# Weight units of a fused attention and two-MLP kernel handled in pairs instead of one by one

## The chip, the cores and the metric

One core of one Trainium2 chip runs the whole program. The metric is the device time of one execution in microseconds (us); lower is better. The core's engines work side by side, each through its own list of instructions in order: TensorE (PE, matrix products, with its weight loads as PEld), VectorE (DVE), ScalarE (ACT), GpSimd (POOL), and SyncE (SP), which here issues most of the transfers (DMAs) between the chip's main memory (HBM) and the core's on-chip memory. Products land in PSUM and are evacuated by ACT or DVE.

## The reference, cut to what matters

```python
# q, k, v: (4, 12, 448, 64), all float32 inputs
q_n, k_n = rmsnorm(q, g_q), rmsnorm(k, g_k)
attn = softmax(q_n @ k_n.T / 8)              # per batch and head
x = (attn @ v) -> (1792, 768)                # 1792 = 4 batches of 448 tokens
a, b = x @ w_a, x @ w_b                      # 768 -> 1536, both
x = (a * b) @ w_out                          # 1536 -> 768
h = x @ w_in                                 # 768 -> 2048
g = max(h, 0) + alpha * min(h, 0)
out = g @ w_out2                             # 2048 -> 768
```

The weights arrive as 64-bit numbers. The kernel splits every value, activations and weights, into a float16 high part and a float16 low part and adds three products (high by high, high by low, low by high), so that float32 accuracy is kept.

## The kernel before, in words

Tokens are handled in four batches of 448 columns. Each batch goes through attention and then four stages: "a" (both first products and their gate), "y" (second product), "h" (third, with the activation), "o" (the last). The list `stages` (line 598) gives their order: a0 y0 h0 o0 a1 y1 a2 h1 o1 y2 h2 a3 o2 y3 o2 h3 o3. Attention runs ahead of the stages as a generator, `att_steps`; batch 0 of it runs alone at the start, and the rest is interleaved, so many steps per stage (`RATE`, line 1258). Three late stages (`FAST`: o2, y3, o3) use a seven-product block scheme with weights formed in advance (`form_weights`, `form_block`).

Each stage is a row of *chains*: 18 or so matmuls of 128x448 that fill one PSUM bank. Weights come in *units*, one per chain in stages a and h (128 columns by 768 rows), two per chain in y and four in o. The list `stream` (lines 715 to 723) holds all units of all stages in order. In stage a, units alternate between w_a and w_b: line 1066 loops over f and, inside, over the two matrices.

The first time a unit is used (76 units, all in a0, y0, h0 and o0), it passes four steps:

- `w_load` (line 729) fetches it as 64-bit numbers into a buffer of pool `raw`, with runs of 128 columns (1 KB).
- `w_convert` (754) turns 64 bits into float32 by an ACT activation (764), a DVE shift (767) and a DVE combine (770), and sums the squares with an ACT activation (778, with a second small ACT instruction that reads the accumulator out).
- `w_scale` (786) adds the squares of a group over the partitions by one small PE matmul into the tile `tot` (`total`, line 127) and makes a power-of-two scale by three DVE instructions (`power`, 112). A group is two units in a and h, the two or four units of a chain in y and o.
- `w_split` (825) makes the high part on ACT (831) and the low part on DVE (832), and stores both to HBM (835).

Later stages fetch the split unit back with one DMA (744), or, in `FAST` stages, formed units (738).

`advance(u)` (847) runs after each unit of the stream; the table `STEPS` (839) says how many units ahead each step goes: load 12, convert 8, scale 6, split 3; refetches go 4 ahead. The pools that matter: `raw` 5 buffers, `wf` (float32 units, also the formed ones) 6, `wh` (split units) 5, `slot` (activations, 35 of 128x2x448 float16), `tmp` 3, and three PSUM banks for chains. While `state["pin"]` holds (attention of batch 0) loads keep their written place in SP's list; most other instructions are ordered by the compiler's own scheduling pass, so the order on an engine can differ from the order in the code.

Two first tiles of attention, `early`, take two of the `raw` buffers during batch 0. The block stages take `raw` buffers for their activations (`blocks`, line 942).

Attention of batches 1 to 3 writes k and q as float16 pairs (`prep3`, `prep4`) and turns them by DMA transposes on SP (lines 355 and 358, into qT and kT), a copy makes qS (361, 362), the probabilities are turned by DMA transposes too (490, into pT), and `scores` (399) then uses kT, qT and qS on PE.

Of the kernel before, what the change touches and what calls it, by code (L numbers as in the profile page):

```python
# [8 lines left out]
F32 = mybir.dt.float32  # L9
F16 = mybir.dt.float16  # L10
# [9 lines left out]
def attention_gated_mlps_kernel(  # L20
# [24 lines left out]
    SLOTS = 35  # L45
# [25 lines left out]
    def slot32(name):  # L71
# [6 lines left out]
    kd0 = keep_p.tile([128, 2 * KB * D], F32, name="kd0")  # L78
# [15 lines left out]
    cgf = const.tile([128, KF2], F32, name="cgf")  # L94
# [8 lines left out]
        "a": const.tile([128, 2 * KF], F32, name="inv_a"),  # L103
        "y": const.tile([128, KD], F32, name="inv_y"),
        "h": const.tile([128, KF2], F32, name="inv_h"),
# [165 lines left out]
    def prep2f(g):  # L271
        d = P[g]
        kr, r = d["kr"], d["rk"]
        kd = kd0[:KP]
        d["kd"] = kd
# [341 lines left out]
    def source(kind, n, part):  # L617
        _, parts, rows = CHAINS[kind]
        w, n = {
            "a": ((w_a, w_b)[n % 2], n // 2), "y": (w_out, n), "h": (w2_in, n), "o": (w2_out, n)  # L620
        }[kind]
        w = w[:, n * 128:(n + 1) * 128]
        if parts == 1:
            return w.rearrange("(k p) f -> p k f", p=128)
# [38 lines left out]
    def form_block(kind, i, j, cols):  # L663
# [3 lines left out]
        def raw():  # L667
            return raw_p.tile([128, 784], I64, tag="raw", name="raw")

        def load():  # L670
            d["x"] = x = raw().bitcast(F16)[:, 0:8 * w].rearrange("p (q l n) -> p q l n", q=4, l=2)
# [5 lines left out]
        def whole(q):  # L677
            if q == 0:
                d["r"] = raw().bitcast(F32)[:, 0:4 * w].rearrange("p (q n) -> p q n", q=4)
# [45 lines left out]

    def size(kind):
        return CHAINS[kind][2] * 128

    def w_load(u):
# [3 lines left out]
        if key[-1] == "s":  # L733
            kind, i, (f, j), _ = key
            t = wf_p.tile([128, 768], F32, tag="wf", name="ws").bitcast(F16)
            t = t[:, 0:2 * WIDE[kind]].rearrange("p (l n) -> p l n", l=2)
            tc.keep_in_program_order(
                nc.sync.dma_start(out=t, in_=form_source(kind, i, f, j))
            )
            w16[u] = t  # L740
            return
        if key in scratch:
            t = wh_p.tile([128, 2, 768], F16, tag="w16", name="w16")[:, :, 0:n]
            nc.sync.dma_start(out=t, in_=scratch[key])
            w16[u] = t
            return
# [616 lines left out]
```

## Time and profile before

| what | value |
|---|---|
| median of 3 runs | 1222.59 us (1215.45 to 1223.43) |
| the profiled execution | 1215.08 us |
| its span from first to last instruction | 1213.0 us |
| PE busy | 1145.4 us (94%) |
| DVE busy | 816.5 us (67%) |
| ACT busy | 770.1 us (63%) |
| POOL busy | 108.2 us (9%) |
| moved by DMA | 269.78 MB, mean 222 GB/s |

Busy time is the union of the instructions of an engine. An instruction's time in the profile runs from its start until its results are written, and the next one on ACT or DVE may start before that, so the sum of the times of single instructions is more than the engine's busy time. A matmul's end is modelled.

### The profile page before, as it was taken

The numbers are of one execution on the slowest core, as the hardware profiler recorded it, in microseconds if no ns is written. First come the engines' busy times: TensorE is split into PE (matmuls) and PEld (weight loads), VectorE is DVE, ScalarE is ACT, GpSimd is POOL, SyncE is SP. The second block draws the span as 40 slices with busy tenths as digits, with TensorE's granted clock in tenths as the row PEclk, the third lists the DMA queues.
The fourth block names the chain that finished last, engine by engine and source line by source line (L and its number), as shares of the span: only waits on it lengthen the run. The fifth ranks groups of instructions, "written<-read, shape, count | busy, mean of one in ns | idle before, by whom it ended". The sixth has DMA issues, their size and how long they took to land. (4 is left out here: it accounts for less than half of the span.)

```text
span 1213.0 us, 20078 instructions
## 1 busy us (share of the span) xinstructions
PE 1145.4 (94%) x7144; PEld 650.6 (54%) x7144; DVE 816.5 (67%) x1695; ACT 770.1 (63%) x1543; POOL 108.2 (9%) x176
## 2 busy tenths in 40 slices
PE   6997999899989799998999999999999999999997
PEld 3553554445434344444445554544555558996597
DVE  7898999999899666677754376554356677523631
ACT  7998999999899666767534366564255335513532
POOL 1000000000001000000012100122200562000000
PEclk9997999999989899998999999999999999999999
DMA  7658999999999999987985677898834798873465
GB/s 190 174 163 211 315 326 329 288 298 305 309 246 308 252 237 253 248 199 173 198 225 152 159 175 164 199 222 190 228 117 135 247 299 284 272 210 107 129 188 171
DMA packets 319267, 269.78 MB, mean 222 GB/s; under 512 B 178464, under 2 KB 275232, under 8 KB 319168
## 3 DMA queue, kind: packets, MB, share of 16 engines
q1 hardware_dynamic: 311376, 246.41, 75.9%
q0 software_dynamic: 7792, 22.10, 6.3%
q8 instruction: 56, 0.92, 0.3%
q14 instruction: 43, 0.35, 0.1%
HBM read 179.77 MB, written 43.25 MB: 184 GB/s over the span
## 5 line engine op out<-in xcount | busy, mean ns | idle before, releaser
L110 PEld LDWEIGHTS <-w 128*128 128x128 f16 x4104 | 398.2, 99 | 393.5 <-issue 39.6
L110 PE MATMUL p<-x,w 128*128 128x448 f16 x1728 | 336.3, 354 | 0.5 <-DVE ab L1080 0.4
L110 PE MATMUL p<-y,w 128*128 128x448 f16 x1152 | 221.6, 352 | 1.4 <-DVE t L1187 1.3
L110 PEld LDWEIGHTS <-ws 128*128 128x128 f16 x1386 | 132.5, 98 | 3.3 <-DMA ws<-f_o_S 2.7
L110 PE MATMUL p<-ab,w 128*128 128x448 f16 x648 | 129.7, 359 | 1.3 <-ACT ab L894 1.2
L110 PE MATMUL p<-g,w 128*128 128x448 f16 x576 | 119.8, 362 | 4.6 <-ACT g L1172 3.5
L421 DVE TENSOR_REDUCE nm<-s 128x2 f32<-128x896 f32 x84 | 91.2, 1086 | 33.5 <-PE s L110 33.3
L483 ACT ACTIVATE p<-pf,ri 128x448 f16<-128x448 f32 x126 | 81.8, 665 | 35.9 <-DMA pT<-p 27.4
L484 DVE SCALAR_TENSOR_TENSOR p<-pf,ri,p 128x448 f16<-128x448 f32 x126 | 84.6, 680 | 28.1 <-ACT p L483 28.0
L110 PE MATMUL l<-g,ws 128*128 128x224 f16 x960 | 94.2, 259 | 1.8 <-DMA ws<-f_o_S 1.8
L438 ACT ACTIVATE pf<-s,nm,esc 128x448 f32<-128x448 f32 x126 | 90.0, 719 | 1.4
L832 DVE SCALAR_TENSOR_TENSOR w<-wf,sc,w 128x768 f16<-128x768 f32 (+1 forms) x76 | 70.1, 929 | 2.5 <-ACT w L831 2.1
L831 ACT ACTIVATE w<-wf,sc 128x768 f16<-128x768 f32 (+1 forms) x76 | 65.4, 869 | 2.6 <-DMA sc_h<-w 1.7
L764 ACT ACTIVATE wf<-raw 128x768 f32<-128x768 f32 (+1 forms) x76 | 63.6, 843 | 5.2 <-DMA raw<-in_moe_w_out_dram 3.2
L770 DVE SCALAR_TENSOR_TENSOR wf<-raw,wf 128x768 int32<-128x768 int32 (+1 forms) x76 | 65.7, 868 | 0.3
L1083 ACT ACTIVATE junk<-ab 128x448 bf16<-128x448 f32 x48 | 27.6, 574 | 59.8 <-DVE ab L1080 59.6
L778 ACT ACTIVATE junk<-wf 128x768 bf16<-128x768 f32 (+1 forms) x76 | 59.3, 781 | 1.3 <-DVE wf L770 1.3
L707 POOL DMA_DIRECT2D f_o_S<-raw x48 | 33.8, 807 | 292.6 <-DVE raw L703 214.0
L110 PE MATMUL s<-kT,qT 128*64 128x448 f16 x252 | 48.3, 375 | 11.6 <-DMA kT<-k 9.1
L1080 DVE SCALAR_TENSOR_TENSOR ab<-p,inv_a,t 128x448 f32<-128x448 f32 x48 | 32.5, 678 | 29.6 <-PE p L110 29.0
L110 PE MATMUL s<-early 128*128 128x448 f32 x84 | 39.6, 598 | 10.0 <-ACT pf L438 9.0
L110 PE MATMUL s<-kT,qS 128*64 128x448 f16 x252 | 46.7, 365 | 2.4 <-DMA qS<-qT 2.4
(171 smaller groups left out, 1434.1 us busy)
## 6 DMA issues: line engine op xcount, KB each, us to landing
w<-sc_a SPq DMA_DIRECT2D x72, 384.0 KB, 3.7
w<-sc_h SPq DMA_DIRECT2D x48, 384.0 KB, 3.1
raw<-in_moe_w_in_dram SPq DMA_DIRECT2D x16, 768.0 KB, 7.3
raw<-in_moe_w_out_dram SPq DMA_DIRECT2D x24, 512.0 KB, 6.1
ws<-f_o_S SPq DMA_DIRECT2D x48, 256.0 KB, 3.8
raw<-in_moe_w_a_dram SPq DMA_DIRECT2D x12, 768.0 KB, 7.3
raw<-in_moe_w_b_dram SPq DMA_DIRECT2D x12, 768.0 KB, 6.5
sc_a<-w SPq DMA_DIRECT2D x24, 384.0 KB, 7.3
```

Of the source, the lines that this page charges most:

```text
L110: nc.tensor.matmul(out=o, lhsT=a, rhs=b, start=first, stop=last)
L421: nc.vector.tensor_reduce(out=nm, in_=ps[:, :, 0:S], axis=AX.X, op=ALU.max, negate=True)
L438: nc.scalar.activation(out=pf, in_=ps[:, j, 0:S], func=AF.Exp, bias=nm[:, j:j + 1], scale=scale[j], accum_out=su[:, j:j + 1],)
L483: nc.scalar.activation(out=t[:, 0, :, 0:KP], in_=pf, func=AF.Copy, scale=r)
L484: nc.vector.scalar_tensor_tensor(out=t[:, 1, :, 0:KP], in0=pf, scalar=r, in1=t[:, 0, :, 0:KP], op0=ALU.mult, op1=ALU.subtract,)
L707: nc.gpsimd.dma_start(out=formed[kind, i, name, j][:, :, cols], in_=d["x"][:, q])
L764: nc.scalar.activation(out=t, in_=hi.bitcast(F32), func=AF.Prelu, scale=2.0 ** -112, alpha=-(2.0 ** 32))
L770: nc.vector.scalar_tensor_tensor(out=ti, in0=lo, scalar=29, in1=ti, op0=ALU.logical_shift_right, op1=ALU.bitwise_or)
L778: nc.scalar.activation(out=junk(768, size(kind)), in_=t, func=AF.Square, accum_out=sums[0][:, j:j + 1])
L831: nc.scalar.activation(out=w[:, 0], in_=t, func=AF.Copy, scale=s)
L832: nc.vector.scalar_tensor_tensor(out=w[:, 1], in0=t, scalar=s, in1=w[:, 0], op0=ALU.mult, op1=ALU.subtract)
L1080: nc.vector.scalar_tensor_tensor(out=ab, in0=ps, scalar=i, in1=t, op0=ALU.mult, op1=ALU.mult)
```

## The change

Two neighbouring units become one pair: in stages a and h two chains that lie side by side (for a: two chains of w_a, then two of w_b), in y and o two parts of the same chain. A pair has one tile in each pool, one instruction per step instead of two, and one scale. For that:

- Stages a and h fetch a raw pair by one DMA with runs of 256 columns; y and o by two DMAs into one tile. Split pairs are stored and refetched by one DMA each. Formed units of the `FAST` stages share tiles in pairs too, alternately from `wf` and `wh`, with a DMA for each.
- Stage a goes through its units as w_a, w_a, w_b, w_b, so that two `tmp` tiles are held at a time.
- Pools: `raw` 3 pairs (was 5 units), `wf` 3 pairs (was 6), `wh` 3 pairs (was 5), `slot` 33 (was 35). The two `early` tiles share one raw pair; `blocks` hands out halves of one raw pair; `form_block` takes both its tiles from one. `kd0` goes; its tile now comes from pool `one`, tag k16.
- Loads go 11 units ahead while pinned and 13 after; formed units 6 ahead (was 5). The tile that takes the unused squares is 8-bit.

The diff, cut to its core:

```diff
-    SLOTS = 35
+    SLOTS = 33
-    raw_p = ctx.enter_context(tc.tile_pool(name="raw", bufs=5))
+    raw_p = ctx.enter_context(tc.tile_pool(name="raw", bufs=3))
-    wf_p = ctx.enter_context(tc.tile_pool(name="wf", bufs=6))
-    wh_p = ctx.enter_context(tc.tile_pool(name="wh", bufs=5))
+    wf_p = ctx.enter_context(tc.tile_pool(name="wf", bufs=3))
+    wh_p = ctx.enter_context(tc.tile_pool(name="wh", bufs=3))
...
-    early = [raw_p.tile([128, 784], I64, tag="raw", name=f"early{i}").bitcast(F32) for i in range(2)]
+    early = raw_p.tile([128, 2, 784], I64, tag="raw", name="early").bitcast(F32)
+    early = [early[:, i] for i in range(2)]
...
     def source(kind, n, part):
-            "a": ((w_a, w_b)[n % 2], n // 2), ...
+            "a": ((w_a, w_b)[n // 2 % 2], n // 4 * 2 + n % 2), ...
+        if parts == 1:
+            w = w[:, n * 128:(n + 2) * 128]
+            return w.rearrange("(k p) f -> p k f", p=128)
...
     def w_load(u):
-        t = raw_p.tile([128, 784], I64, tag="raw", name="raw")[:, 0:n]
-        i = nc.sync.dma_start(out=t.rearrange("p (k f) -> p k f", f=128), in_=source(*key))
+        t = raw_p.tile([128, 2 * 784], I64, tag="raw", name="raw")[:, 0:2 * n]
+        for j, x in enumerate(members[u]):
+            if j and key[0] in "ah":
+                break
+            if key[0] in "ah":
+                at = t.rearrange("p (k f) -> p k f", f=256)
+            else:
+                at = t[:, j * n:(j + 1) * n].rearrange("p (k f) -> p k f", f=128)
+            i = nc.sync.dma_start(out=at, in_=source(*stream[x]))
...
     def w_convert(u):
-        t = wf_p.tile([128, 768], F32, tag="wf", name="wf")[:, 0:size(kind)]
+        t = wf_p.tile([128, 2 * 768], F32, tag="wf", name="wf")[:, 0:2 * size(kind)]
...
     def w_scale(u):
-        us = range(u - parts * chains + 1, u + 1)
-        sc = sm_p.tile([128, 2], F32, tag="sc", name="sc")[:, 0:chains]
-        power(total(squares.pop(u), len(us), chains), sc, iv, 2)
+        us = [u - 2, u][2 - sq.shape[1]:]
+        sc = sm_p.tile([128, 1], F32, tag="sc", name="sc")
+        power(total(sq, len(us)), sc, inv[kind][:, m:m + 1], 2)
...
     def w_split(u):
-        nc.scalar.activation(out=w[:, 0], in_=t, func=AF.Copy, scale=s)
+        nc.scalar.activation(out=hi, in_=t, func=AF.Copy, scale=s)
-        nc.sync.dma_start(out=scratch[stream[u]], in_=w)
+        nc.sync.dma_start(out=whole[stream[u]], in_=w)
...
-    STEPS = [(w_load, 12), (w_convert, 8), (w_scale, 6), (w_split, 3)]
+    STEPS = [(w_load, 11), (w_convert, 8), (w_scale, 6), (w_split, 3)]
...
     def stage_a(b):
-        for f in range(KF):
-            for w in range(2):
+        for n in range(2 * KF):
+            f, w = n // 4 * 2 + n % 2, n // 2 % 2
```

## Rows read from the trace of the kernel before

**Rows 1.** The page: busy time of two engines.
```profile
PE 1145.4 (94%) x7144; PEld 650.6 (54%) x7144; DVE 816.5 (67%) x1695; ACT 770.1 (63%) x1543; POOL 108.2 (9%) x176
```
**Rows 2.** Stretches (us): engines' busy time and instructions, granted clock, DMA share, GB/s.
```profile
core 0: us, PE busy (x) PEld busy (x) DVE busy (x) ACT busy (x) POOL busy (x), PEclk, DMA share, GB/s
36.00:116.00 80.00, 66.95 (x391) 38.90 (x388) 70.95 (x205) 76.04 (x168) 0.00 (x0) 0.92 0.61 172
...
116.00:430.00 314.00, 287.65 (x1617) 144.53 (x1617) 281.29 (x593) 288.74 (x585) 9.09 (x13) 0.97 1.09 297
...
390.00:430.00 40.00, 32.24 (x176) 15.21 (x176) 25.71 (x60) 29.24 (x65) 5.77 (x8) 0.87 1.04 256
...
560.00:1213.00 653.00, 643.53 (x4257) 393.70 (x4254) 345.32 (x614) 288.44 (x528) 92.69 (x144) 1.00 0.70 194
```
**Rows 3.** Waits of PE from 116 to 430: us in total, times, longest.
```profile
PE s L110 <- DMA kT<-k: 8.5, 3, 5.4
PE p L110 <- ACT g L1172: 3.5, 1, 3.5
PE tot L110 <- ACT sq L375: 2.3, 1, 2.3
PE tot L110 <- DVE x L535: 2.2, 2, 1.6
...
PE tot L110 <- DVE tots L135: 0.7, 1, 0.7
```
**Rows 4.** Timeline of ACT in a0: start, us, line, what.
```profile
160.54 0.95 ACT L831 ACTIVATE w<-wf,sc 128x768 f16<-128x768 f32 x1
161.37 0.86 ACT L778 ACTIVATE junk<-wf 128x768 bf16<-128x768 f32 x1
162.10 0.22 ACT L778 ACTIVATION_READ_ACCUMULATOR junk<-wf 128x1 f32 x1
162.19 0.92 ACT L764 ACTIVATE wf<-raw 128x768 f32<-128x768 f32 x1
162.98 0.65 ACT L1077 ACTIVATE t<-p,inv_a 128x448 f32<-128x448 f32 x1
```
**Rows 5.** Timeline of ACT in o0, with units of 512.
```profile
389.14 0.75 ACT L831 ACTIVATE w<-wf,sc 128x512 f16<-128x512 f32 x1
389.75 0.70 ACT L764 ACTIVATE wf<-raw 128x512 f32<-128x512 f32 x1
390.31 0.66 ACT L778 ACTIVATE junk<-wf 128x512 bf16<-128x512 f32 x1
390.83 0.24 ACT L778 ACTIVATION_READ_ACCUMULATOR junk<-wf 128x1 f32 x1
390.92 0.70 ACT L483 ACTIVATE p<-pf,ri 128x448 f16<-128x448 f32 x1
```
**Rows 6.** Timeline of DVE, in a0 and in o0.
```profile
159.52 0.95 DVE L770 SCALAR_TENSOR_TENSOR wf<-raw,wf 128x768 int32<-128x768 int32 x1
160.40 1.00 DVE L832 SCALAR_TENSOR_TENSOR w<-wf,sc,w 128x768 f16<-128x768 f32 x1
161.32 0.18 DVE L267 SCALAR_TENSOR_TENSOR r<-t,r 128x30 f32<-128x30 f32 x1
...
385.26 0.75 DVE L832 SCALAR_TENSOR_TENSOR w<-wf,sc,w 128x512 f16<-128x512 f32 x1
385.92 0.68 DVE L770 SCALAR_TENSOR_TENSOR wf<-raw,wf 128x512 int32<-128x512 int32 x1
386.53 0.68 DVE L484 SCALAR_TENSOR_TENSOR p<-pf,ri,p 128x448 f16<-128x448 f32 x1
```
**Rows 7.** Issues that write kT from 116 to 430, with issue-to-landing time.
```profile
L358 SPq DMA_TRANSPOSE kT<-k x7: 1230/2361/3911, 116.1 to 428.8; - x7
...
DMA to landing us min/median/max: 3.0/5.6/7.7
```
**Rows 8.** The same from 430 to 840, after the last unit is converted.
```profile
DMA to landing us min/median/max: 2.9/3.6/7.2
```
**Rows 9.** The page: issues by what they move, KB each, median us to landing.
```profile
w<-sc_a SPq DMA_DIRECT2D x72, 384.0 KB, 3.7
raw<-in_moe_w_a_dram SPq DMA_DIRECT2D x12, 768.0 KB, 7.3
```
**Rows 10.** Timeline of PE at the first chain of stage o1.
```profile
756.00 4.34 PE L110 MATMUL p<-g,w 128*128 128x448 f16 x22
```

More of the change, by code (lines that the diff above doesn't have):

```diff
@@ L741, in w_load @@
+            for j, x in enumerate(members[u]):
+                kind, i, (f, c), _ = stream[x]
+                w = t[:, j, 0:2 * WIDE[kind]].rearrange("p (l n) -> p l n", l=2)
+                tc.keep_in_program_order(
+                    nc.sync.dma_start(out=w, in_=form_source(kind, i, f, c))
+                )
+                w16[x] = w.rearrange("p l (k f) -> p l k f", f=128)
             return
         if key in scratch:
-            t = wh_p.tile([128, 2, 768], F16, tag="w16", name="w16")[:, :, 0:n]
@@ new lines, in w_load @@
+            nc.sync.dma_start(out=t, in_=whole[key])
+            give(u, t)
+            return
+        t = raw_p.tile([128, 2 * 784], I64, tag="raw", name="raw")[:, 0:2 * n]
+        whole[key] = hbm.tile(
+            [128, 2, 2 * n] if key[0] in "ah" else [128, 2, 2, n], F16, name=f"sc_{key[0]}{key[1]}_{key[2]}"
+        )
+        for j, x in enumerate(members[u]):
+            scratch[stream[x]] = None if key[0] in "ah" else whole[key][:, j]
+            if j and key[0] in "ah":
+                break
+            if key[0] in "ah":
+                at = t.rearrange("p (k f) -> p k f", f=256)
+            else:
+                at = t[:, j * n:(j + 1) * n].rearrange("p (k f) -> p k f", f=128)
+            i = nc.sync.dma_start(out=at, in_=source(*stream[x]))
+            if state["pin"]:
+                tc.keep_in_program_order(i)
@@ L751, in w_load @@
         raws[u] = t
-        scratch[key] = hbm.tile([128, 2, n], F16, name=f"sc_{key[0]}{key[1]}_{key[2]}")
+    whole = {}
     def w_convert(u):
@@ L773, in w_convert @@
         wf[u] = t
[L774 to L775 removed]
+        pairs = 2 if kind == "o" else 1
+        j = PARTS[4].index(part) // 2 if kind == "o" else 0
         if j == 0:
[L777 removed]
+            sums[0] = sm_p.tile([128, 2], F32, tag="ss", name="ss")
         nc.scalar.activation(
[L779 removed]
+            out=junk(1536, 2 * size(kind)), in_=t, func=AF.Square, accum_out=sums[0][:, j:j + 1]
         )
[L781 to L782 removed]
+        if j == pairs - 1:
+            squares[u] = sums[0][:, 0:pairs]
     sums, squares = [None], {}
@@ L843, in attention_gated_mlps_kernel @@
     firsts = [u for u, key in enumerate(stream) if key[-1] != "s" and not (key in seen or seen.add(key))]
-    again = sorted(set(range(len(stream))) - set(firsts))
+    firsts = [u for u in firsts if u in members]
+    again = sorted(x for x in set(members) - set(firsts))
     at = [[0] * len(STEPS), [0] * len(AGAIN)]
@@ L852, in advance @@
                     x = todo[done[i]]
-                    if x > u + ahead + (stream[x][-1] == "s") or (f is w_split and x not in scales):
+                    extra = 2 * (stream[x][-1] == "s" or f is w_load and steps is STEPS and not state["pin"])
+                    if x > u + ahead + extra or (f is w_split and x not in scales):
                         break
@@ L940, in form_steps @@
             f += [x[:, :, j] for j in range(j1 - j0)]
+    other = []
     def blocks():
-        r = raw_p.tile([128, 784], I64, tag="raw", name="raw").bitcast(F32)
-        r = r.rearrange("p (j n) -> p j n", j=7)
+        if not other:
+            r = raw_p.tile([128, 2, 784], I64, tag="raw", name="raw").bitcast(F32)
+            other.extend([r[:, 1], r[:, 0]])
+        r = other.pop().rearrange("p (j n) -> p j n", j=7)
         return r, (r[:, 0:3:2], r[:, 3:5])
@@ L1165, in one @@
                 nc.scalar.activation(
[L1166 removed]
+                    out=rs[i][1][j], in_=halves_of(t), func=AF.Copy, scale=cgf[:, f // 2:f // 2 + 1]
                 )
```

143 lines of the change are left out of this document (79 added, 64 removed).

## The prediction

> **What bounds the kernel now.** I began with the busy time of the whole span [rows 1]: PE is busy 94%, which leaves 67.6 us of the 1213.0 us span idle. That share is a mean over unlike stages, so the next view is the table of stretches [rows 2]. From 560 us to the end PE is busy 643.5 of 653 us at a granted clock of 1.00, while DVE and ACT have half their time free. No unit is converted there, and there are under 10 us to win. From 36 to 116 us, attention of batch 0 with the first weights beside it, ACT is busy 76.0 of 80 us and PE only 66.9: ACT bounds. From 116 to 430 us, where a0, y0, h0 and o0 convert nearly all of the 76 units, three engines are nearly level: PE 287.7 of 314 us, ACT 288.7, DVE 281.3. PE idles 26.3 us there, and a granted clock of 0.97 (of the full 2.4 GHz; the other level is 1.2) costs another 0.03 x 314 = 9.4 us. This stretch is what the change touches.
>
> The waits of PE in this stretch [rows 3] say who ends the 26 us. Thirteen rows, of which the first and the last are shown, sum to 26.0 us: 9.4 us are ended by a DMA (kT 8.5, qS 0.9), 10.6 by ACT, 6.0 by DVE. Most sit at the seams of stages, single gaps of 1 to 5 us, and not at every weight unit.
>
> **What one merged instruction saves.** The duration of an instruction overlaps the next, so what counts is the distance from its start to the start of the next in a row of them without idle time. ACT with 768 columns [rows 4]: split 161.37 - 160.54 = 0.83 us, squares 0.73, read-out 0.09, convert 0.79. With 512 columns [rows 5]: split 0.61, convert 0.56, squares 0.52, read-out 0.09. The difference over 256 columns gives a slope, and the rest is the part paid per instruction: split 0.61 - 2 x 0.22 = 0.17, convert 0.56 - 2 x 0.23 = 0.10, squares 0.52 - 2 x 0.21 = 0.10, read-out 0.09 whole. A pair saves one of each: 0.46 us on ACT. DVE [rows 6]: the combine goes 0.88 (768) and 0.61 (512), the low part 0.92 and 0.66, fixed parts 0.07 and 0.14; the shift I take like the combine, 0.07, an estimate. A pair saves 0.28 us on DVE. For all 38 pairs that is 17.5 us of ACT and 10.6 us of DVE. From durations instead of distances one would get about twice as much; that would count the overlap as work.
>
> The Trainium skill, page "VectorE: DVE Perf Modes", section "The TRN2 errata", says that VectorE and ScalarE pay a fixed latency per instruction which tiles of 512 elements or more amortize. By that rule little would be left to win here, since the units have 512 and 768 columns already; the rows above give it its number, about 0.1 us per instruction.
>
> **The sum.** About 34 of the 38 pairs fall into 116 to 430 us (10 units are converted and 5 split earlier, a few split later). There ACT loses 34 x 0.46 = 15.6 us and DVE 9.5 us. Neither is alone on the path: PE has 287.7 us of its own work, which nothing here shortens. So the freed time only shrinks the waits that ACT and DVE end. I let a wait behind an engine shrink as its free time grows: ACT's goes from 25.3 to 40.9 us, so its 10.6 us of waits become 10.6 x 25.3 / 40.9 = 6.6, a gain of 4.0; DVE's free time goes from 32.7 to 42.2, its 6.0 become 4.6, a gain of 1.4. That is 21% of the idle time, and I give back the same share of the 9.4 us of slow clock: 2.0. Together 7.4 us. The bounds: nothing, if the waits are lengths of chains and not queues; all of it, 16.6 us and its share of the clock, 6.0, together 22.6. I take the model's value, since most of these waits are single gaps at stage seams, where the chain has a length of its own.
>
> From 36 to 116 us ACT bounds: five pairs' convert, squares and read-out (0.29 each) and two pairs' splits (0.17) are 1.8 us, minus the split of a fourth unit that pairing pulls ahead, 0.83. I take 1.0 us, with bounds 0 and 1.8.
>
> **The rest, at nothing, with its cover.** One small matmul and three small DVE instructions per group stay, 32 groups before and after; only y loses a reduction. The group of a pair still has two units of PE work between squares and scale. Its chain is longer (convert 1.5, DVE 2.4, squares 1.4 us instead of about half), and two units are 7 us; if ACT is behind by more than 1.5 us, the small matmul comes late, and behind it in PE's list stand the chains. Three pairs in each pool give the same lead as five or six units, because a step now frees two units at once. The order w_a, w_a, w_b, w_b holds two of three `tmp` tiles; ACT evacuates twice and then DVE twice, covered by three PSUM banks. Refetches of 768 KB replace two of 384 KB that land in 3.7 us [rows 9]; even twice that is within two pairs, 14 us. 33 slots: at the end of h1, 6 Y, 12 AB, 14 G and the first X of batch 3 fill them, so the last two G wait for the last chain; o1 first needs them in its third unit, 24 matmuls of 0.2 us later [rows 10], 4.7 us that hide them. Without that cover, 2.7 us. The 8-bit tile for squares has no row of its own: nothing either way, bound by the 0.73 us of the squares, which go with columns. Raw runs of 256 columns halve the packets of 40 units; PE never waits for raw data in [rows 3], so nothing, with a gain hidden in the bound of the kT waits.
>
> Forecast: 1215.08 (profiled; its span is 1213.0 plus 2.1 around it) - 7.4 - 1.0 = 1206.7. That execution lies 7.5 us under the median of the runs; set against the median, 1222.59 - 8.4 = 1214.
>
> **Rivals.** *Slower, by transfers that stand in line.* kT transposes land in 5.6 us while weights stream [rows 7] and in 3.6 us afterwards [rows 8]: 2.0 us behind weight traffic. Raw pairs and stores now come in bursts twice as long, so this may double. PE already waits for three of the seven kT; if the cover of all is gone, 7 x 2.0 = 14 us. From 390 to 430 us, around the 5.4 us wait for kT, PE idled 7.8 us and lost 0.13 x 40 = 5.2 us by the clock, 0.67 us for each idle us [rows 2]; that adds 9. Against the gain of 8: 1222.6 + 15 = 1238. It decides from about 0.6 us of added lateness per kT on. Against it: raw pairs of a and h have half the packets, and SP issues fewer DMAs.
>
> The Trainium skill, page "DMA: Bandwidth & Descriptors", section "Queues, rings and completion order", says that on each DMA engine the descriptors of a queue are consumed in ring order, which speaks for this rival. The trace agrees as far as 5.6 against 3.6 us go; whether longer bursts lengthen it no row shows.
>
> *Larger gain.* All waits that ACT and DVE end from 116 to 430 us vanish, 22.6 us with the clock, and 1.8 before: 1198. For it: ACT and DVE are over 89% busy there, where a little relief goes far. Against: seams have chains of their own.
>
> *No effect.* The waits are chain lengths; longer single instructions give back what fewer save, since an evacuation behind a pair's split waits 1.5 instead of 0.8 us: 1222.
>
> **How the numbers follow.** Forecast (1208 to 1218) 0.40, larger gain (1190 to 1208) 0.22, no effect (1218 to 1230) 0.17, slower (1230 to 1245) 0.21. Over or under 1%, 12.2 us, is about what a measurement of this kernel can tell from no change: faster than 1210.4 are the larger gain and a third of the forecast, 0.35; slower than 1234.8 most of the last, and a reshuffled order that I can't price, 0.20; within, 0.45. The range 1192 to 1236 leaves out 0.05 below and 0.12 above; the forecast's own is 1208 to 1218.
>
> **What would show it.** ACT busy from 116 us to the last conversion falls by some 15 us and DVE by 9; PE's waits on ACT and DVE there fall by a third; convert shows as 128x1536 at about 1.6 us. Wrong, if kT lands later than 6 us and PE waits more than 8.5 us for it, if the small `tot` matmuls wait on squares at many units, or if PE waits at the end of h1.

## The result and the profile after

The kernel after takes 1224.62 us (median of 14 runs, 1220.57 to 1229.43) against 1215.48 us of the kernel before beside it (14 runs): a ratio of 1.0074, with a 95% interval of 1.0053 to 1.0095. The change makes the kernel slower by 0.7%, where the forecast had it faster by 0.7%. The time lies in the range 1192 to 1236, on the other side of no change, and in the part of it that the forecast gave to "no effect" (1218 to 1230, a chance of 0.17). The profiled execution took 1229.43 us, 4.8 more than the median, so not all of the differences below are the kernel's.

The page of after, busy time of the engines, as [rows 1]:

```profile
PE 1146.7 (93%) x7144; PEld 655.0 (53%) x7144; DVE 805.2 (66%) x1575; ACT 755.6 (62%) x1391; POOL 113.9 (9%) x176
```

ACT works 14.5 us less and DVE 11.3 us less, as the sum had it (17.5 and 10.6 over all pairs). PE is busy within 1.3 us of before, and its idle time grew from 67.6 to 81.0 us. The time freed on two engines did not reach the third.

The table of stretches of after, on the borders of [rows 2]:

```profile
core 0: us, PE busy (x) PEld busy (x) DVE busy (x) ACT busy (x) POOL busy (x), PEclk, DMA share, GB/s
36.00:116.00 80.00, 64.49 (x376) 36.15 (x374) 69.60 (x195) 75.28 (x152) 0.00 (x0) 0.95 0.50 152
116.00:430.00 314.00, 288.36 (x1610) 148.52 (x1607) 270.26 (x479) 272.06 (x440) 8.10 (x13) 0.95 1.01 293
```

From 116 to 430 us ACT is busy 272.1 instead of 288.7 us and DVE 270.3 instead of 281.3, while PE idles 25.6 instead of 26.3 at a granted clock of 0.95 instead of 0.97. So the free time grew as the sum had it: ACT's from 25.3 to 41.9 us (forecast 40.9), DVE's from 32.7 to 43.7 (forecast 42.2). PE's idle time did not follow. But fixed borders hold different work by now. So here are both kernels cut where the work changes: up to the end of a0, then y0 to o0, then a1 (each cut is the first matmul of a stage's first chain). The same view, first of before:

```profile
0.00:219.00 219.00, 189.09 (x1109) 104.28 (x1110) 195.44 (x496) 203.27 (x429) 5.91 (x16) 0.97 0.86 244
219.00:438.00 219.00, 195.91 (x1099) 96.56 (x1099) 187.53 (x400) 192.48 (x392) 8.41 (x13) 0.95 1.09 285
438.00:553.30 115.30, 110.21 (x660) 53.01 (x657) 81.53 (x176) 79.23 (x184) 1.08 (x4) 0.97 1.02 232
```

and of after:

```profile
0.00:227.80 227.80, 193.39 (x1110) 105.73 (x1111) 192.84 (x448) 200.56 (x366) 5.45 (x16) 0.96 0.76 235
227.80:441.20 213.40, 193.50 (x1093) 98.49 (x1093) 178.65 (x326) 180.13 (x301) 7.91 (x12) 0.95 1.04 288
441.20:569.00 127.80, 110.48 (x665) 53.79 (x663) 82.06 (x177) 80.14 (x186) 1.07 (x4) 0.99 0.98 217
```

The first stretch is 8.8 us longer, the second 5.6 shorter, a1 12.5 longer; behind a1 the two are equal within 1 us (659.7 and 658.7). In a1 nothing is converted: ACT and DVE do the same work in both kernels (79 to 82 us), and PE idles 17.3 instead of 5.1 us. The largest part of the loss sits in a stretch for which the forecast had no term.

PE's waits from 116 to 430 us, as [rows 3], the first four of sixteen rows:

```profile
PE x L110 <- DVE pw L117: 6.2, 2, 3.5
PE p L110 <- ACT w L886: 3.1, 1, 3.1
PE s L110 <- DMA kT<-k: 2.4, 2, 1.4
PE tot L110 <- ACT junk L827: 2.2, 1, 2.2
```

In all sixteen rows ACT ends 11.9 us, DVE 10.9 and a DMA 2.7; before it was 10.6, 6.0 and 9.4. The waits for ACT and DVE grew from 16.6 to 22.8 us, where the sum had them shrink to 11.2. PE's idle time stayed level only because its waits for transfers fell. This is more than the noise of one execution: before_slots33 and before_qk4, below, which have nearly or wholly the order of before, show 16.4 and 16.0 us of waits for ACT and DVE here, and after_qk4 and after_raw128, with that of after, 21.0 and 19.9.

PE waits 2.4 us for kT, not 8.5 or more, and kT lands after 4.7 us (median) instead of 5.6 [rows 7]: the rival of late kT did not come. Twice PE waits for `pw`, an instruction of the scale's chain, once for the squares (`junk`) and once for a split (`w`), so that chain is late at a few places, not at many units. This is the longer wait for `pw`, on DVE and then on PE:

```profile
308.35 1.82 DVE L887 SCALAR_TENSOR_TENSOR w<-wf,sc,w 128x1536 f16<-128x1536 f32 x1 [0.22 <-ACT w L886]
310.09 1.75 DVE L819 SCALAR_TENSOR_TENSOR wf<-raw,wf 128x1536 int32<-128x1536 int32 x1
311.75 0.15 DVE L117 TENSOR_SCALAR pw<-tot 128x1 int32<-128x1 int32 x1
...
311.96 0.57 PE L110 MATMUL x<-pT,v 112*64 112x448 f16 x4 [3.45 <-DVE pw L117]
```

`pw` reads the small product `tot` out of the only buffer of a PSUM pool (`ps_x`) that attention's products `x` use too. It takes 0.15 us, but it stands behind two merged instructions of 1.8 us each, and PE stands behind it. From the start of a0 to the end of o0 the products `x` wait 6.2 us for the instruction that reads `tot` (`pw`, or `tots` where it adds columns first). In the six kernels with single units it is 0.5 to 3.2 us, in after_ops1, below, which has pairs but single instructions, 3.0, and in the thirteen with merged DVE instructions 1.4 to 7.7.

The timeline of ACT in a0, as [rows 4], now with pairs:

```profile
141.15 1.56 ACT L886 ACTIVATE w<-wf,sc 128x1536 f16<-128x1536 f32 x1
142.62 0.56 ACT L1144 ACTIVATE junk<-ab 128x448 uint8<-128x448 f32 x1
...
143.79 1.47 ACT L827 ACTIVATE junk<-wf 128x1536 uint8<-128x1536 f32 x1
145.16 0.18 ACT L827 ACTIVATION_READ_ACCUMULATOR junk<-wf 128x1 f32 x1
...
145.77 1.59 ACT L813 ACTIVATE wf<-raw 128x1536 f32<-128x1536 f32 x1
147.27 0.65 ACT L482 ACTIVATE p<-pf,ri 128x448 f16<-128x448 f32 x1
```

From start to next start a pair's split takes 142.62 - 141.15 = 1.47 us, its squares 1.37, its convert 1.50. Twice the single ones less the fixed parts of the prediction would be 1.49, 1.36 and 1.48. The price of a merged instruction was right.

Who waits for whom in a0: the waits of DVE, before (us in total, times, longest):

```profile
DVE wf L767 <- ACT wf L764: 2.0, 3, 0.9
DVE w L832 <- ACT w L831: 1.3, 3, 0.6
```

and of DVE and ACT, after:

```profile
DVE wf L816 <- ACT wf L813: 7.7, 8, 2.4
DVE w L887 <- ACT w L886: 2.6, 2, 1.8
...
ACT junk L827 <- DVE wf L819: 3.4, 5, 1.0
```

The steps of a pair hand over between the two engines: ACT converts, DVE shifts and combines, ACT squares; ACT makes the high part, DVE the low part. With units of their own, one engine works on the next unit while the other takes over. With one instruction for both, the other engine stands until all of it is done. Rows of this kind grow from 3.3 to 13.7 us in a0. In all of a0, DVE's waits for ACT grow from 4.1 to 11.5 us and ACT's for DVE from under 1 to 6.6; from y0 to o0, DVE's go from 18.3 to 31.1. What these waits cost the kernel is another question, which after_ops1 and after_load10 bear on below.

In a1 the waits of ACT for attention's transfers stand out. Before:

```profile
ACT sq L375 <- DMA vn<-in_v_dram: 6.2, 3, 4.0
ACT sk L236 <- DMA kr<-in_k_dram: 4.8, 3, 2.6
```

After, the same, and then the timeline around the longest wait for kr (start, duration, engine, line, and in brackets the idle time before it and what ended that):

```profile
ACT sk L236 <- DMA kr<-in_k_dram: 11.5, 4, 4.8
...
ACT sq L374 <- DMA vn<-in_v_dram: 6.0, 1, 6.0
```

```profile
467.37 0.69 DVE L355 TENSOR_TENSOR k<-kr,k 112x512 f16<-112x512 f32 x1
...
488.62 0.42 SPq L206 DMA_DIRECT2D kr<-in_k_dram  x1
...
493.92 0.63 ACT L236 ACTIVATE sk<-kr 112x512 f32<-112x512 f32 x1 [4.81 <-DMA kr<-in_k_dram]
...
494.59 0.69 DVE L240 TENSOR_REDUCE stat<-sk 112x8 f32<-112x512 f32 x1 [5.80 <-ACT sk L236]
...
508.26 3.57 PE L110 MATMUL p<-x,w 128*128 128x448 f16 x18 [2.25 <-DVE ab L1141]
```

A tile for k (`kr`) had been free since 468.1 us (the end of the first row, the instruction that reads it last), but SP asks for its data only at 488.62. ACT stands 4.8 us at `sk`, with softmax and evacuations behind it on its list, and DVE 5.8 us at `stat`. PE goes on for some chains; then attention's work arrives in a heap, and from 501 us on PE waits for evacuations that stand behind it. At 505.3 another `kr` tile is freed and asked for at 516.4.

### The profile page after: what moved, and what is told of

Same layout as the page of the kernel before. It is cut to its first block, busy times and chain, and to the rows that moved or that the text cites. A ratio compares the mean times of both kernels' runs of the same rounds, so it can differ in the third digit from the quotient of the medians.

```text
span 1227.7 us, 19413 instructions
## 1 busy us (share of the span) xinstructions
PE 1146.7 (93%) x7144; PEld 655.0 (53%) x7144; DVE 805.2 (66%) x1575; ACT 755.6 (62%) x1391; POOL 113.9 (9%) x176
## 2 busy tenths in 40 slices
DMA packets 279871, 269.74 MB, mean 220 GB/s; under 512 B 176192, under 2 KB 229952, under 8 KB 279776
## 5 line engine op out<-in xcount | busy, mean ns | idle before, releaser
L110 PEld LDWEIGHTS <-w 128*128 128x128 f16 x4776 | 462.6, 99 | 408.7 <-issue 51.9
L110 PE MATMUL p<-g,w 128*128 128x448 f16 (+1 forms) x588 | 119.8, 357 | 6.3 <-ACT w L886 3.1
L482 ACT ACTIVATE p<-pf,ri 128x448 f16<-128x448 f32 x126 | 81.3, 663 | 49.4 <-DMA pT<-p 40.9
L483 DVE SCALAR_TENSOR_TENSOR p<-pf,ri,p 128x448 f16<-128x448 f32 x126 | 84.3, 680 | 34.5 <-ACT p L482 34.4
L110 PEld LDWEIGHTS <-ws 128*128 128x128 f16 x714 | 68.5, 98 | 0.4
L887 DVE SCALAR_TENSOR_TENSOR w<-wf,sc,w 128x1536 f16<-128x1536 f32 (+1 forms) x38 | 62.6, 1647 | 7.3 <-ACT w L886 7.2
L813 ACT ACTIVATE wf<-raw 128x1536 f32<-128x1536 f32 (+1 forms) x38 | 56.0, 1473 | 13.4 <-DVE g L1248 2.6
L1144 ACT ACTIVATE junk<-ab 128x448 uint8<-128x448 f32 x48 | 27.4, 571 | 59.5 <-DVE ab L1141 59.5
L819 DVE SCALAR_TENSOR_TENSOR wf<-raw,wf 128x1536 int32<-128x1536 int32 (+1 forms) x38 | 60.3, 1586 | 0.2
L827 ACT ACTIVATE junk<-wf 128x1536 uint8<-128x1536 f32 (+1 forms) x38 | 51.3, 1351 | 7.2 <-DVE wf L819 6.0
L110 PE MATMUL x<-pT,v 112*64 112x448 f16 x432 | 47.5, 372 | 8.1 <-DVE pw L117 6.2
L886 ACT ACTIVATE w<-wf,sc 128x1536 f16<-128x1536 f32 (+1 forms) x38 | 54.5, 1435 | 0.2 <-DMA sc_o<-w 0.2
L110 PE MATMUL l<-g,ws 128*128 128x224 f16 x480 | 49.6, 259 | 0.0
```

Source lines behind the costliest of these rows:

```text
L110: nc.tensor.matmul(out=o, lhsT=a, rhs=b, start=first, stop=last)
L482: nc.scalar.activation(out=t[:, 0, :, 0:KP], in_=pf, func=AF.Copy, scale=r)
L483: nc.vector.scalar_tensor_tensor(out=t[:, 1, :, 0:KP], in0=pf, scalar=r, in1=t[:, 0, :, 0:KP], op0=ALU.mult, op1=ALU.subtract,)
L813: nc.scalar.activation(out=t, in_=hi.bitcast(F32), func=AF.Prelu, scale=2.0 ** -112, alpha=-(2.0 ** 32))
L819: nc.vector.scalar_tensor_tensor(out=ti, in0=lo, scalar=29, in1=ti, op0=ALU.logical_shift_right, op1=ALU.bitwise_or)
L827: nc.scalar.activation(out=junk(1536, 2 * size(kind)), in_=t, func=AF.Square, accum_out=sums[0][:, j:j + 1])
```

## The experiments

All 18 kernels were timed beside the kernel before. The table cuts each profile as above; the next to last column is the sum of ACT's waits for transfers in a1. How much single executions differ can be read from two pairs: before_qk4 and after_load12_qk4 have the instruction order of before and of after_load12 on PE, DVE, ACT and POOL, with seven or eight DMAs at other places on SP. They differ by 4.3 us in the column y0 to o0 and by at most 1.6 in the two beside it.

| kernel | to end of a0 | y0 to o0 | a1 | ACT waits | ratio to before (95%) |
|---|---|---|---|---|---|
| before | 219.0 | 219.1 | 115.4 | 15.9 | |
| before_slots33 | 218.3 | 215.1 | 115.4 | 15.1 | 0.9998 (0.9976 to 1.0020) |
| before_qk4 | 219.0 | 214.9 | 115.3 | 14.9 | 1.0002 (0.9979 to 1.0024) |
| before_aabb | 220.5 | 211.7 | 117.4 | 19.1 | 1.0000 (0.9976 to 1.0025) |
| before_storefirst | 220.3 | 212.0 | 117.0 | 19.2 | 0.9978 (0.9953 to 1.0002) |
| before_load11 | 221.7 | 215.5 | 119.2 | 22.7 | 1.0021 (1.0004 to 1.0038) |
| after | 227.8 | 213.4 | 127.8 | 27.9 | 1.0074 (1.0053 to 1.0095) |
| after_qk4 | 227.8 | 209.1 | 128.0 | 27.6 | 1.0080 (1.0052 to 1.0108) |
| after_raw128 | 226.3 | 209.5 | 128.9 | 27.4 | 1.0084 (1.0051 to 1.0117) |
| after_storefirst | 224.3 | 208.0 | 128.6 | 32.4 | 1.0075 (1.0049 to 1.0102) |
| after_ops1 | 218.5 | 220.6 | 128.2 | 25.6 | 1.0038 (1.0019 to 1.0057) |
| after_wh6 | 217.6 | 221.7 | 130.1 | 37.2 | 1.0069 (1.0041 to 1.0097) |
| after_refetch1 | 219.6 | 213.9 | 126.6 | 32.2 | 1.0001 (0.9977 to 1.0025) |
| after_abab | 228.3 | 213.5 | 126.7 | 33.6 | 1.0125 (1.0100 to 1.0149) |
| after_attpool | 228.1 | 217.3 | 132.6 | 37.8 | 1.0194 (1.0166 to 1.0222) |
| after_load13 | 228.8 | 218.6 | 121.2 | 23.2 | 1.0086 (1.0056 to 1.0116) |
| after_load12 | 227.5 | 203.2 | 117.4 | 16.5 | 0.9953 (0.9929 to 0.9977) |
| after_load12_qk4 | 229.1 | 207.5 | 117.0 | 16.6 | 0.9975 (0.9950 to 0.9999) |
| after_load12_attpool | 226.6 | 205.3 | 126.7 | 30.5 | 1.0087 (1.0053 to 1.0120) |
| after_load10 | 217.9 | 206.6 | 122.0 | 22.7 | 0.9920 (0.9892 to 0.9947) |

The first theories were: (1) the order w_a, w_a, w_b, w_b of stage a, (2) refetches of 768 KB, (3) two slots less, (4) the compiler's scheduling pass, which orders all instructions anew for any edit.

**The order of stage a, alone and undone.** In before_aabb, the kernel before with the new order; in after_abab, the kernel after with the old one (a pair is then w_a and w_b of one f, its raw data two DMAs of 128 columns).

```diff
-            "a": ((w_a, w_b)[n % 2], n // 2), ...
+            "a": ((w_a, w_b)[n // 2 % 2], n // 4 * 2 + n % 2), ...
```

> The kernel before with one edit: stage a takes its units as w_a, w_a, w_b, w_b; units stay single. In the changed kernel stage a1, which converts nothing, is 12.5 us longer in the trace (127.8 against 115.3 us), and PE waits there 7.3 us for the evacuation of its own chains, which before were none. Theory 1 (the order of stage a: two DVE evacuations in a row behind a DVE backlog use up the PSUM banks): ratio to before 1.006 to 1.010, a1 122 to 128 us, the same chain waits. Theory 2 (refetches of 768 KB delay the small loads of attention, k and q, on the same queue): ratio 1.000 within 0.002, a1 115 us. Theory 3 (two slots fewer): 1.000. Theory 4 (no part by itself; the compiler's order of instructions falls differently with any edit): anything from 0.995 to 1.007.

> The changed kernel with the order of stage a undone: w_a, w_b in turn, a pair is one unit of each, its raw halves come by two DMAs of 128 columns; all else as changed. Theory 1: 1215 to 1217 us, ratio 0.998 to 1.002, a1 back near 115 us. Theory 2: stays at 1223 to 1226, ratio about 1.007. Theory 3: about 1.007. Theory 4: anything between 0.997 and 1.010.

Theory 1 falls twice: the new order alone costs nothing that could be measured, a1 is 117.4 us; with the old order the pairs are slower still, a1 is 126.7.

**Refetch by single units.** after_refetch1 asks for each unit of a pair by itself, the second one a unit later. For that the halves of a pair lie one behind the other, and with it DVE makes the low part of a pair of a and h by two instructions instead of one.

```diff
-            nc.sync.dma_start(out=t, in_=whole[key])
+            nc.sync.dma_start(out=t, in_=scratch[key])
```

> The changed kernel with the refetch of a split pair cut into one DMA per unit, the second issued one unit later (384 KB each instead of 768 KB in one), the pair's tile as changed; for that the split pair lies unit by unit in its tile, and in stages a and h the low part is two DVE instructions (20 times one more, about 3 us of DVE). Theory 2: ratio to before 0.999 to 1.002, a1 near 116 us, k loads land as before (3.8 us). Theory 1 and theory 3: stays at 1.006 to 1.009. Theory 4: anything.

The loss is gone, 1217.02 us, but not where theory 2 has it: a1 stays at 126.6 us, and the 8.2 us come back ahead of the end of a0, where no unit is refetched. What came back may belong to the split, below, or to the order of the instructions, which this edit shifts too.

**Two slots less,** in the kernel before.

```diff
-    SLOTS = 35
+    SLOTS = 33
```

> The kernel before with 33 slots for activations instead of 35. Theory 3: ratio 1.005 or more, with waits of PE in h1 or in a1. Theories 1 and 2: 1.000 within 0.002. Theory 4: a shift of either sign by up to 0.005, since the compiler orders again.

1214.92 us, and no stage changes by more than single executions do: theory 3 falls, and the prediction's step on the slots holds.

**Parts of the pairing undone.** after_ops1 keeps pairs in buffers and transfers, but convert, squares and split go by two instructions of half a pair each. after_wh6 converts in pairs, but splits, stores and refetches single units, in six tiles. after_raw128 fetches a raw pair by two DMAs.

```diff
# after_ops1
+        for e in range(2):
+            c = slice(e * m, e * m + m)
...
-                out=t, in_=hi.bitcast(F32), func=AF.Prelu, ...
+                out=t[:, c], in_=hi[:, c].bitcast(F32), func=AF.Prelu, ...
# after_wh6
-    wh_p = ctx.enter_context(tc.tile_pool(name="wh", bufs=3))
+    wh_p = ctx.enter_context(tc.tile_pool(name="wh", bufs=6))
# after_raw128
-            w = w[:, n * 128:(n + 2) * 128]
+            w = w[:, n * 128:(n + 1) * 128]
```

> The kernel after, pairs kept in buffers and transfers, but convert, squares and split done by two instructions of one unit each, as before. By the theory that a merged instruction of 1.5 to 1.8 us holds up the evacuations behind it: a0 falls from 107.8 to about 103, and ACT's busy time rises by some 14 us and DVE's by some 11 to the values of before; ratio about 1.003. By the theory that the pair grain of buffers and transfers is the cause: stages stay within 2 us of those of after, and the o0 gain (95.0 against 101.0) is lost by the added busy time, so the ratio is 1.010 to 1.014. By the theory of a shifted order: a1 takes any value between 115 and 128.

> The kernel after, but split, store and refetch go by single units again, into six tiles of one unit in place of three of two; load and convert stay in pairs. By the theory that the pair grain of the 16-bit tiles (a tile comes free only when both units are through, so the next pair is asked for later) is what lengthens a1: a1 falls from 127.8 to about 116 us, the whole to a ratio of 0.995 to 1.000. By the theory that the loss in a1 comes from the order in which the attention's steps are queued, which any edit shifts: a1 has no reason to go back, 125 to 128 us. By the theory of longer merged instructions (convert, squares stay merged): a0 stays at about 108, o0 at about 96.

> The kernel after, but a raw pair of the first and third stage is fetched by two DMAs of 128-column runs, as before. By the theory that the long runs of 256 columns crowd other transfers (kr, vn, kT) out: start falls from 120.0 to 115.9 and a0 from 107.8 to about 104; a1, where no raw pair is fetched, stays. By the theory that run length costs nothing: all stages within 2 us of after, or longer by what the doubled number of packets of these pairs costs, ratio 1.007 to 1.012.

after_ops1, waits of DVE in a0:

```profile
DVE wf L819 <- ACT wf L816: 0.8, 3, 0.4
```

With single instructions the handover at the convert falls from 7.7 to 0.8 us, the one at the split (2.6) has no row left, PE's products `x` wait 3.0 instead of 6.2 us for the reader of `tot`, and the first stretch goes from 227.8 back to 218.5. ACT and DVE are busy 770.3 and 819.1 us again, and y0 to o0 is 7.2 us longer than in after. It is tempting to call the 9.3 us the price of the longer handovers. But here is a0 alone, first of after, then of after_ops1:

```profile
120.00:227.80 107.80, 100.11 (x560) 52.37 (x558) 93.02 (x158) 95.35 (x147) 0.19 (x1) 0.96 0.96 301
111.30:218.50 107.20, 101.88 (x574) 52.96 (x573) 101.38 (x211) 102.64 (x203) 0.95 (x1) 0.96 1.02 305
```

It is as long with single instructions (the expectation had about 103), though it then holds 16 matmuls of scores that after runs ahead of a0. The difference lies ahead of a0, where ACT and DVE wait for each other equally long (9.6 and 9.4 us in sum). Up to the end of a0 PE idles 34.4 us in after and 28.0 in after_ops1. The three kernels in which the low part of a pair of a and h is not one DVE instruction (ops1, wh6, refetch1) all end a0 at 217.6 to 219.6; with lead 11 the other kernels with pairs end it at 224.3 to 228.3. But after_load10, below, has that instruction whole and 11.3 us of waits between the two engines in a0 (after 18.1, before 4.8), and ends a0 at 217.9. So the longer waits come from the merged instructions, and what they cost up to the end of a0 is not shown.

Run length costs and wins nothing: after_raw128 moves 295551 packets instead of 279871 in the same time. None of the three changes a1: 128.2, 130.1, 128.9. The grain of the split tiles, long instructions and long runs are each ruled out as its only cause.

**The lead of the loads.** `(w_load, 11)` is 12, 13 and 10 in after_load12, after_load13 and after_load10, and before_load11 has 11 in place of 12.

```diff
-    STEPS = [(w_load, 11), (w_convert, 8), (w_scale, 6), (w_split, 3)]
+    STEPS = [(w_load, 12), (w_convert, 8), (w_scale, 6), (w_split, 3)]
```

> The kernel after with the lead of the loads at 12 units in place of 11, a change of one number that moves only when a raw pair is asked for. In a1 no raw pair is loaded. By the theory that the loss is structural (buffers, transfers, long instructions): all stages within 2 us of after, a1 127 to 128, ratio 1.006 to 1.009. By the theory of a shifted order: single stages move by several us without a cause in the pairs, start between 110 and 120, a1 between 115 and 128, ratio 1.000 to 1.015.

> The kernel after with the lead of the loads at 13 in place of 11. Between 11 and 12 o0 fell from 95.0 to 85.3 and a1 from 127.8 to 117.4 us. By the theory that an earlier raw pair is what helps (raw data come too late at 11): as with 12 or better, o0 83 to 87, a1 115 to 118, ratio 0.990 to 0.997. By the theory that the order of the whole shifts with any edit: o0 anywhere from 85 to 102 and a1 either near 117 or near 128, ratio 0.995 to 1.010.

> The kernel before with the lead of the loads at 11 units in place of 12, no pairs. By the theory that the order of the whole shifts with any edit, whatever it is for: stages start to a1 move by several us, a1 between 115 and 128, ratio 0.995 to 1.012. By the theory that pairs are the cause: a1 stays at 115 to 117, ratio 0.998 to 1.003.

> The kernel after with the lead of the loads at 10. With 11 and 13 a raw pair is asked for in the same unit as a split's store, with 10 and 12 in the unit between, with the convert. By the theory that raw loads and stores of 1.5 MB in one unit stand in each other's way: as 12, o0 84 to 88, a1 115 to 119, ratio 0.992 to 0.998. By the theory that the compiler's order falls one way or another with each edit: o0 85 to 102, a1 115 to 128, with no relation to even or odd, ratio 0.995 to 1.010.

after_load10, the first stretch and a1:

```profile
0.00:217.90 217.90, 188.16 (x1110) 105.84 (x1111) 193.03 (x450) 199.45 (x366) 5.43 (x16) 0.96 0.81 252
...
424.50:546.50 122.00, 109.73 (x661) 53.43 (x659) 81.37 (x176) 78.35 (x183) 0.83 (x4) 0.98 0.98 217
```

One number moves this kernel from 0.7% slower to 0.5% (lead 12) or 0.8% faster (lead 10: 1205.03 against 1213.90 us), and lead 13 leaves it at 0.9% slower. With all that belongs to the pairs unchanged, a1 goes to 117.4 and 122.0, though no raw unit is loaded in it. The loss is not a property of the pairs as such. The single units move less: lead 11 costs them 0.2% and 3.8 us of a1. That the order of the instructions goes with a1, and not chance, shows where it is the same: on ACT and DVE after_raw128 has the order of after throughout and after_qk4 has it but for some 25 places, and their a1 takes 128.9 and 128.0 us; before_qk4 and after_load12_qk4, with the orders of before and after_load12, repeat their a1 within 0.4. Between before and after a quarter of the instructions of ACT and DVE in a1 change their place in the order. Nor does every edit shift it: before_slots33 and after_raw128 leave it all but as it was.

**The order on SP from a0 to o0.** With leads 11 and 13 a raw pair is asked for in the unit in which a split is stored, with 10 and 12 in the unit between. On SP's list 32 of the 38 stores of after stand right behind a raw pair (lead 13: 21, 12: 15, 10: 12); in before it is 59 of 76 stores (the expectations say 73). after_storefirst and before_storefirst keep the lead but ask for raw data last in a unit.

```diff
-            for i, (f, ahead) in enumerate(steps):
+            for i, (f, ahead) in sorted(enumerate(steps), key=lambda z: z[1][0] is w_load and not state["pin"]):
```

> The kernel after with its lead of 11, but within a unit the raw pair is asked for last, behind the split's store, in place of first. On SP's list 32 of the 38 stores of the kernel after stand right behind a raw pair (before: 59 of 73, raws of half the size; lead 13: 21, lead 12: 15, lead 10: 12); here 10 do. In the trace of after those stores land after 9.2 to 10.2 us (a, y, h), with leads 10 and 12 after 4.9 to 8.2, and SP spends 263 us issuing from a0 to o0 against 222 and 198. By the theory that a raw pair of 1.5 MB, a store and the pT transposes in one file on SP cost the loss: stores land after 5 to 8 us, SP's issue time from a0 to o0 falls to 200 to 230, ratio 0.989 to 0.998. By the theory that lead 10 or 12 helps by when the raw data come, or by chance: ratio 1.003 to 1.010.

> The kernel before with the same order within a unit, raw asked for behind the store: 35 of 73 stores stand right behind a raw unit instead of 59. The control, single units at the better order. By the theory of the file on SP it gains something too, less than the pairs, since its raws are 768 KB: ratio 0.992 to 0.999, and what pairs bring by themselves is the difference of the two kernels so ordered. If the order within a unit is worth nothing here: 0.998 to 1.002.

Issues of stores from 112 to 430 us, KB each and median us to landing, after:

```profile
sc_a<-w SPq DMA_DIRECT2D x10, 768.0 KB, 10.2
sc_h<-w SPq DMA_DIRECT2D x8, 768.0 KB, 9.2
```

and after_storefirst:

```profile
sc_a<-w SPq DMA_DIRECT2D x10, 768.0 KB, 6.9
sc_h<-w SPq DMA_DIRECT2D x8, 768.0 KB, 5.5
```

The stores land 3 to 4 us sooner, as expected, and SP's time in issuing from a0 to o0 falls from 263 to 247 us, less than expected. The ratio stays at 1.0075, a1 at 128.6, and before_storefirst gains nothing that is clear of noise (0.9978, up to 1.0002). So the stores do land later behind a raw pair, but moving them ahead of it does not bring the time back. The Trainium skill, page "DMA: Bandwidth & Descriptors", section "Queues, rings and completion order", says that each DMA engine takes a queue's descriptors in ring order; the 10.2 against 6.9 us agree with that.

**Attention's loads in a1.** after_attpool issues kr, qr, vr and vn of the later batches from POOL's queue; after_load12_attpool has lead 12 beside it. after_qk4, before_qk4 and after_load12_qk4 call `load_qk` one column step earlier from batch 2 on.

```diff
# attpool
-        nc.sync.dma_start(
+        eng = nc.gpsimd if g >= 2 * NP else nc.sync
+        eng.dma_start(
# qk4
-                    if c == 5:
+                    if c == (4 if g >= 2 * NP - 1 else 5):
                         load_qk(g + 3)
```

> The kernel after, but the loads of q, k and v for the batches that a1 and a2 prepare (kr, qr, vr from batch 2 on, vn of batch 3) are issued from POOL's queue in place of SP's; nothing of the pairs is touched. In a1 of the kernel after ACT stands 11.5 us waiting for kr and 6.0 for vn, and PE idles 17.3 us; before it was 4.8, 6.2 and 5.0. By the theory that these loads stand in SP's line behind pT transposes, vn's wait for a free tile and refetches: a1 falls from 127.8 to 115 to 119 us, ACT's waits for kr and vn to under 10 together, ratio 0.996 to 1.000. By the theory that the refetches of 768 KB crowd the transfers themselves: kr lands as late as it does, a1 stays at 126 to 129, ratio 1.006 to 1.009. By the theory that only the order which the compiler happens to choose counts: any value between the two, with the waits in other places.

> Both at once: lead of the loads 12, and the attention loads of later batches from POOL's queue. If the lead of 12 and the other queue cure the same thing, late attention transfers in a1: a1 at 115 to 118, o0 at 85, ratio 0.993 to 0.996, the same as with the lead alone. If they cure different things: below 0.991.

> The kernel after, but from batch 2 on the loads of q and k (kr, qr) are asked for at column step 4 instead of 5, right behind the step that frees their tiles; all that runs before a1 keeps its place in the program. In a1 of the kernel after, two kr tiles were freed at 468.1 and 505.3 us and asked for only at 488.6 and 516.4, 20.5 and 11.1 us later, while SP issued pT transposes and refetches; in the kernel before the same took 6 us at most. By the theory that kr asked for late is what lengthens a1: both delays fall below 6 us, ACT's wait for kr from 11.5 to under 6, a1 to 115 to 120, ratio 0.997 to 1.001. By the theory that the pairs' long refetches hold a1 up wherever kr stands: a1 125 to 129, ratio 1.006 to 1.009, whatever the delay of kr.

> The kernel before with the same earlier kr and qr. There kr is asked for within 6 us of its tile in a1, and a1 has 5.0 us of PE idle time, so by the theory of late kr there is nothing to win: a1 114 to 117, ratio 0.997 to 1.002. By the theory that any edit reshuffles the order: a1 up to 128, ratio up to 1.010.

> The lead of 12 and the earlier kr and qr together. With the lead of 12 kr is asked for within 3.2 us of its tile in a1 already, so by the theory of late kr little is left: a1 115 to 118, ratio 0.992 to 0.997, as with the lead alone. By the theory that every edit reshuffles the order, any of a1 115 to 128, ratio 0.992 to 1.006.

after_attpool in a1: ACT's wait for kr, and, in a view of its own, the issues of kr (KB each, median us to landing):

```profile
ACT sk L237 <- DMA kr<-in_k_dram: 20.2, 5, 6.7
```

```profile
kr<-in_k_dram POOLq DMA_DIRECT2D x5, 224.0 KB, 6.6
```

From POOL's queue kr is asked for within 1.7 us of its tile, but it lands after 6.6 instead of 4.4 us, ACT waits 20.2 us for it, and a1 takes 132.6 us; with lead 12 the same edit takes a1 from 117.4 to 126.7. Taking the loads out of SP's line does not shorten a1, so my theory got no support. It is not refuted either: kr lands later from this queue, and the edit shifts the order of a1 on ACT and DVE as well. The earlier call of `load_qk` did not test the theory: kr is asked for as late as before (27.5 and 20.0 us after its tile was free), so after_qk4 and before_qk4 nearly repeat the orders of after and before, with 128.0 and 115.3 us for a1.

Over all 20 kernels a1 goes with ACT's waits for transfers in it: up to 19.2 us of waits a1 takes 115 to 117 us, at 22.7 to 23.2 us 119 to 122, from 25.6 us on 126 to 133 (correlation 0.94). In after PE idles 12.2 us more in a1 than before, and a1 is 12.4 us longer. The likely way is that ACT, held up by these waits, comes late to evacuate, as the timeline above shows at one place; that the waits cause the length is not shown by a run that removes them alone.

## Why the prediction was wrong

*The price of a merged instruction* was right: 14.5 and 11.3 us of busy time, 1.47, 1.37 and 1.50 us for the instructions of a pair.

*"The freed time only shrinks the waits that ACT and DVE end"* failed first. The free time came as forecast, 41.9 and 43.7 us, but from 116 to 430 us the waits that it was to shrink from 16.6 to 11.2 us grew to 22.8. The model treats ACT and DVE as queues in front of PE, where more free time means shorter waits. It left out that what stands behind a merged instruction may wait twice as long. PE's 6.2 us of waits for `pw` are such a case; with single instructions (after_ops1) the like takes 3.0. The convert and split chains, which cross from ACT to DVE and back, are another: in a0 the rows of these crossings grow by 10.4 us, and ACT's idle time from 3.0 to 12.5 us. The prediction named the longer chain and covered it by the lead ("two units are 7 us"), and named the longer wait behind a pair's split as the rival "no effect", with 0.17. Yet these two do not account for the growth: from 116 to 430 us PE waits 22.0 us for ACT and DVE in after_ops1, without merged instructions, and 14.6 in after_load10, with them. So what sets these waits is open, and the order of the instructions is the likeliest. The clock term failed with the waits: 2.0 us were to come back, and the granted clock fell to 0.95.

From y0 to o0 the kernel is 5.6 us shorter, near the 7.4 of the sum, but that is luck and not its mechanism. PE's waits for ACT and DVE rise there from 13.8 to 18.5 us, and those for transfers, kT above all, fall from 10.0 to 2.7 (over the repeated orders, from 7.4 to 10.0 down to 1.4 to 3.8); why they fall is open. Up to the end of a0 8.8 us went the other way, where 36 to 116 us was to bring 1.0: 4.1 of them before a0 and 4.7 in it, there 1.9 of idle time of PE and 2.8 of busy time, at a granted clock of 0.96 instead of 0.99. How much of this the merged instructions cost is not settled: after_load10 has them too and ends a0 at 217.9.

*"The rest, at nothing"* failed in a1, by the largest part, 12.5 us. The prediction had terms up to 430 us and "under 10 us to win" from 560 us on, and none between. It held a1 for untouched, since nothing is converted there. But as the section on the kernel before says, the compiler orders most instructions, so an edit can move attention's loads and their readers on every list, and this one did. That was the "reshuffled order that I can't price", folded into a chance of 0.20. Its size is in the table: 10.4 us of a1 between leads 11 and 12 of one kernel, and 1.0086 - 0.9920 = 1.7% of the whole, some 20 us, between leads 13 and 10.

*The rival that named the direction*, transfers that stand in line, named a wrong place and a wrong transfer. kT lands sooner (4.7 us) and PE waits 6 us less for it. The transfers that ACT waits for most in a1 are kr, vn and pT.

*Right in the rest*: 33 slots, 128 or 256 columns a run and the order of stage a each cost nothing that could be measured, a1 is as long with refetches of 384 KB as of 768 KB, and o1 takes 71.5 us (before 71.8), so the end of h1 is hidden. The forecast of 8.4 us is about what the pairs bring at lead 10 (8.9 us), but the terms do not bear it out there either: the waits for ACT and DVE are 14.6 us, not 11.2.

*Open* is which property of the order lengthens a1. Late requests for kr come along with it. In the eight kernels with pairs, lead 11 and all loads on SP, the request that stands at 488.62 in the timeline comes 16 to 23 us after its tile is free, and a1 takes 126 to 130 us; in the ten with a1 under 123 the same request comes at most 7.2 us late. But taking the loads to another queue did not cure it, and a run that moves these requests alone and leaves the other lists as they are is missing.

## What to carry to other kernels

When one instruction takes the place of two, count what stands behind it as well as the fixed costs: the next step of a chain that crosses engines, or a short instruction that another engine waits for. Busy time that is saved need not shorten a wait. When a compiler orders the work, time a change together with its neighbours in a harmless number, such as a lead, before it is judged: here the same change is worth between -0.8% and +0.9%. And look for the loss by stages cut at the work, also in stages that the change does not touch.

## What the runs showed of the hardware

A transfer of 224 KB issued from POOL's queue landed after 6.6 us (median in a1 of after_attpool), the same from SP after 4.4 us (after), though it no longer stood behind SP's other work. Stores of 768 KB landed after 10.2 us (median of ten) in after, where most stand right behind a raw load of up to 1536 KB, and after 6.9 us in after_storefirst, where most do not. PE waited 3.45 us for an instruction of 0.15 us on DVE (`pw`) that stood behind two of 1.8 us. The number of packets, 279871 or 295551, made no difference that could be measured (after, after_raw128).
